# Tiles of the first pair beside the last batch: nine gathered instead of five, W_in earlier, W_out between the first units

## The chip, the core and the metric

The kernel runs on one core of a Trainium2 chip. The core has TensorE (PE, matrix products into PSUM), VectorE (DVE), ScalarE (ACT), GpSimd (POOL, which works on SBUF only) and SyncE (SP, which here issues every transfer). Each engine takes its instructions strictly in the order of its own queue and waits on semaphores for the others. The metric is the device time of one execution in microseconds (us), lower is better.

## What is computed

Three stages over 8 batches of 576 rows: an attention over 32 memory slots with 8 heads of 64, whose heads together are 512 columns; a first MLP of 512 to 2048 to 512 with a layer norm ahead and a residual; and a gated MLP. The change concerns the gated MLP and its loads:

```python
def _moe2_ref(x, w_in, g_ln, w_sg, b_sg, w_out):
    h = x @ w_in                                   # 512 -> 1024
    h = 0.5 * h * (1.0 + np.tanh(c * (h + 0.044715 * h ** 3)))
    u, v = (h[..., :d_ff // 2], h[..., d_ff // 2:])
    v_n = (v - mu) / np.sqrt(var + 1e-06) * g_ln   # over the 512 columns of v
    v_s = np.einsum('ts,bsd->btd', w_sg, v_n) + b_sg[None, :, None]
    gated = u * v_s
    return (x + gated @ w_out).astype(np.float32)
```

All weights and inputs arrive as 64-bit or 32-bit floats in DRAM. Products are made from pairs of a high and a low part (three matmuls for one), so every operand is converted and split into two tiles first.

## The kernel before

Phase 1 (`phase1`) is the attention and the first MLP. It goes through the batches one after the other. For each block of rows and each chunk c of the 2048 hidden columns `m1` makes a first-layer product into PSUM (ph, L550), `relu` splits it on ACT (hh, or cr for the 64 rows that belong to a tile shared with the next block, L536) and DVE (hl, L537), and three steps later `m2` adds the second-layer product into the PSUM tile of each row tile (py, L580 to L582). A finished row tile is scaled and added on DVE (L585) and stored to DRAM as y_d. The 36 row tiles have 128 rows; nine of them are a pair of batches, and the fifth of the nine (tile 4) holds 64 rows of each batch.

Phase 2 (`phase2`) is the gated MLP, pair by pair. For each row tile, y is loaded (`y_load`), transposed in blocks of 32 on DVE (`y_turn`, L824) and split (`y_split`: ACT L833, POOL L834). `s2` makes the v half of the first product (pv, 12 matmuls of 512 columns, L857), its gelu (ACT L843 square, DVE L844, ACT L845 tanh, DVE L846), the statistics over columns (DVE L867 to L869, reciprocal root on POOL L86 to L96), the scaling (DVE L871) and the split into vhl (ACT L874, POOL L875; for tile 4 in two parts L882, L883). Then there are 16 units of a pair: `s3` makes the u half (pu, 12 matmuls of 288 columns, L940) and its gelu; `s4` multiplies W_sg with all vhl of a batch (pvs, 14 matmuls of 288, L965), gates it (DVE L967, POOL L968) and splits it (ACT L970, POOL L971). In the loop the `s3` of a unit is written two units ahead of its `s4`. PSUM has two tiles for pu and two for pvs. `s5` makes the last product (po, L988), adds y (DVE L990) and stores.

W_in and W_out arrive as 64-bit floats. `load_piece` fetches a piece of 128 rows in two halves of 256 KB into tiles raw, of which there are three; `convert_piece` calls `split`: for each half ACT L108, DVE L109 and L110 make 32-bit floats of the words; for W_in ACT L122 and POOL L123 then make the two parts, for W_out, which is also scaled by 0.5, ACT L125 and DVE L126. Pieces 0 to 7 are W_in (its v half first), 8 to 11 W_out.

To keep PE busy at the change of phases, the table `ahead` hangs work of phase 2 on the steps of the last batch (`begin_phase2`): the chunks of W_sg, the pieces, and for the first five tiles of the first pair load, turn, split and `s2`. A list scheduler then orders each engine's instructions by its own estimate of when they are ready, so the order of instructions is not quite that of the code; the conversions, turns and splits carry an order edge (`issue_after`) behind the relu of the step.

## Time and profile before

| | us |
|---|---|
| median of 3 runs | 1232.28 |
| lowest and highest run | 1230.69, 1232.63 |
| the profiled execution | 1230.81 |
| its span, first to last instruction | 1229.0 |
| PE, DVE, ACT, POOL busy | 1182.6, 694.7, 467.4, 399.3 |
| mean granted clock of TensorE, share of full | 0.986 |

The last batch runs to about 805 us of the span, the gated MLP from there. PE matmuls overlap, so a busy time adds up ends that are modelled; how fast PE goes is read from the starts of its matmuls, one after the other. In a timeline row, what stands in brackets is the idle time ahead of the instruction and the instruction that ended it. An instruction's duration can hold a wait that no semaphore shows.

### The profile page before, as it was taken

The numbers are of one execution on the slowest core, as the hardware profiler recorded it, in microseconds if no ns is written. First come the engines' busy times: TensorE is split into PE (matmuls) and PEld (weight loads), VectorE is DVE, ScalarE is ACT, GpSimd is POOL, SyncE is SP. The second block draws the span as 40 slices with busy tenths as digits, with TensorE's granted clock in tenths as the row PEclk, the third lists the DMA queues.
The fourth block names the chain that finished last, engine by engine and source line by source line (L and its number), as shares of the span: only waits on it lengthen the run. The fifth ranks groups of instructions, "written<-read, shape, count | busy, mean of one in ns | idle before, by whom it ended". The sixth has DMA issues, their size and how long they took to land.

```text
span 1229.0 us, 20976 instructions
## 1 busy us (share of the span) xinstructions
PE 1182.6 (96%) x7711; PEld 988.0 (80%) x7711; DVE 694.7 (57%) x1669; ACT 467.4 (38%) x1064; POOL 399.3 (32%) x621
## 2 busy tenths in 40 slices
PE   4699899999999999999999999999999999999998
PEld 2376678878888778878878788788989988998997
DVE  2887565654744536645545545774576467447632
ACT  2565333223332323323223435543354354444430
POOL 2123212211211211201111103346586475657641
PEclk9699999999999999999999999999999999999999
DMA  9998764464534374343432233340141043023202
GB/s 207 270 247 244 196 177 111 102 167 124 138 94 120 89 217 87 97 141 82 125 119 70 71 98 104 94 132 1 52 140 42 10 127 97 1 70 95 78 18 69
DMA packets 204518, 138.85 MB, mean 113 GB/s; under 512 B 95104, under 2 KB 176128, under 8 KB 204416
## 3 DMA queue, kind: packets, MB, share of 16 engines
q1 hardware_dynamic: 204416, 137.51, 40.5%
q8 instruction: 61, 1.00, 0.3%
q14 instruction: 41, 0.34, 0.1%
HBM read 114.40 MB, written 31.33 MB: 119 GB/s over the span
## 4 chain that ended last, share of the span: by engine, by line
PE 82%; DVE 5%; DMA 5%; issue 3%; SPq 3%; ACT 1%; POOL 1%; DVEq 0%; POOLq 0%; ACTq 0%
PE ph L550 14%; PE pvs L965 10%; PE py L580 9%; PE py L582 9%; PE py L581 9%; PE po L988 8%; PE pu L940 8%; PE pv L857 7%; DMA raw<-in_moe_w_ch_dram 3%; SPq L81 3%; PE pvw L496 3%; PE kvp L294 2%; DMA q<-q_d 1%; PE sc L374 1%; PE px L430 1%
## 5 line engine op out<-in xcount | busy, mean ns | idle before, releaser
L550 PE MATMUL ph<-aTh,vw 128*128 128x320 f32 (+1 forms) x1024 | 246.4, 301 | 3.4 <-ACT vw L507 1.4
L580 PE MATMUL py<-whl,hh 128*128 128x512 f32 x512 | 205.9, 404 | 5.2 <-ACT hh L536 5.0
L581 PE MATMUL py<-whl,hh 128*128 128x512 f32 x512 | 203.3, 397 | 0.0
L550 PEld LDWEIGHTS ph<-aTh,vw 128*128 128x128 f32 x1024 | 177.9, 190 | 29.4 <-issue 8.3
L582 PE MATMUL py<-whl,hl 128*128 128x512 f32 x512 | 187.1, 397 | 0.0
L536 ACT ACTIVATE hh<-ph 128x256 fp32r<-128x256 f32 x256 | 97.5, 384 | 163.6 <-PE ph L550 95.5
L537 DVE SCALAR_TENSOR_TENSOR hl<-ph,hh 128x256 fp32r<-128x256 f32 x256 | 106.9, 422 | 91.4 <-ACT hh L536 89.5
L550 PE MATMUL ph<-aTl,vw 128*128 128x256 f32 (+1 forms) x512 | 152.8, 299 | 0.0
L965 PE MATMUL pvs<-wsh,vhl 128*128 128x288 f32 x576 | 123.5, 298 | 3.8 <-POOL vhl L883 2.7
L580 PEld LDWEIGHTS py<-whl,hh 128*128 128x128 f32 x512 | 97.0, 190 | 33.5 <-ACT hh L536 8.1
L581 PEld LDWEIGHTS py<-whl,hh 128*128 128x128 f32 x512 | 97.5, 190 | 19.8 <-issue 2.3
L940 PE MATMUL pu<-yTh,whl 128*128 128x288 f32 x512 | 111.3, 295 | 0.6 <-DVE ug L846 0.6
L550 PEld LDWEIGHTS ph<-aTl,vw 128*128 128x128 f32 x512 | 97.3, 190 | 10.3 <-issue 2.1
L582 PEld LDWEIGHTS py<-whl,hl 128*128 128x128 f32 x512 | 91.6, 189 | 15.8 <-issue 5.7
L965 PEld LDWEIGHTS pvs<-wsh,vhl 128*128 128x128 f32 x576 | 95.7, 190 | 5.6 <-POOL vhl L883 3.1
L857 PE MATMUL pv<-whl,yTh 128*128 128x512 f32 x288 | 90.9, 396 | 0.9 <-DVE vg L846 0.9
L988 PE MATMUL po<-whl,gh 128*128 128x512 f32 x288 | 90.0, 391 | 0.0
L940 PEld LDWEIGHTS pu<-yTh,whl 128*128 128x128 f32 x512 | 85.3, 188 | 2.0 <-DVE ug L846 1.0
L965 PE MATMUL pvs<-wsl,vhl 128*128 128x288 f32 x256 | 75.9, 297 | 0.0
L940 PE MATMUL pu<-yTl,whl 128*128 128x288 f32 x256 | 75.4, 294 | 0.0
L536 ACT ACTIVATE cr<-ph 128x64 fp32r<-128x64 f32 x128 | 28.4, 223 | 123.3 <-PE ph L550 122.8
L968 POOL TENSOR_TENSOR gt<-gt,ug 128x288 f32<-128x288 f32 x64 | 51.7, 809 | 65.1 <-DVE gt L967 64.9
(153 smaller groups left out, 2162.6 us busy)
## 6 DMA issues: line engine op xcount, KB each, us to landing
wc<-w_d SPq DMA_DIRECT2D x56, 512.0 KB, 4.9
y_d<-x SPq DMA_DIRECT2D x36, 256.0 KB, 2.7
yt<-y_d SPq DMA_DIRECT2D x36, 256.0 KB, 2.7
yr<-y_d SPq DMA_DIRECT2D x36, 256.0 KB, 3.0
kv<-in_k_dram SPq DMA_DIRECT2D x32, 256.0 KB, 4.0
kv<-in_v_dram SPq DMA_DIRECT2D x32, 256.0 KB, 4.2
raw<-in_moe_w_ch_dram SPq DMA_DIRECT2D x32, 256.0 KB, 8.3
raw<-in_moe_w_ch_dram SPq DMA_DIRECT2D x16, 512.0 KB, 7.4
```

Source lines behind the costliest of these rows:

```text
L81: return nc.sync.dma_start(out=out_ap, in_=in_ap)
L536: high = A.activation(out_h, src, AF.Relu)
L537: return high, V.scalar_tensor_tensor(out=out_l, in0=src, scalar=0.0, in1=out_h.bitcast(F32), op0=ALU.max, op1=ALU.subtract)
L550: PE.matmul(ph, w_[:, ks], x[:, g, 0:w], start=(n == 0), stop=(n == 3 * HK - 1))
L580: PE.matmul(py, hh, wh, start=start, stop=False)
L581: PE.matmul(py, hh, wl, start=False, stop=False)
L582: PE.matmul(py, hl, wh, start=False, stop=stop)
L857: PE.matmul(pv, y[:, kc, cs], w, start=(n == 0), stop=(n == 3 * KC - 1))
L940: PE.matmul(pu, w[:, ds_], y[:, kc, cs], start=(n == 0), stop=(n == 3 * KC - 1))
L965: PE.matmul(pvs, v_, w_, start=(n == 0), stop=(n == len(ops) - 1))
L968: G.tensor_tensor(out=gt, in0=gt, in1=ug, op=ALU.mult)
L988: PE.matmul(po, gg[:, dc, cs], w, start=(n == 0), stop=(n == 3 * KC - 1))
```

## The change

A constant `BESIDE = 7` is new. The table hangs only the eight pieces of W_in on the steps, each four steps sooner, and all nine tiles' load, turn and split, with `s2` for the first seven. The split pair of y tiles is allocated at the first `y_split` instead of the first `y_load`. W_out is loaded and converted in the loop of the first eight units, without the order edge; the two `s2` that are left stand behind the first and the third unit there.

```diff
     def convert_piece(p):
-        w = split(R.pop(("piece", p)), wpool, 0.5 if kind == 2 else None, R["relu"])
+        w = split(R.pop(("piece", p)), wpool, 0.5 if kind == 2 else None, None if kind == 2 else R["relu"])
...
-        if X["p"] == 0:
+        if X["p"] == 0 and t < BESIDE:
             z, vg = two(wpool, F32, "vg")
...
-            vh, vl = two(wpool if t < TPP - 2 else R["w3"], F32R, "vhl")
+            vh, vl = two(wpool if t < BESIDE else R["w3"], F32R, "vhl")
...
-    for n in range(len(PIECES)):
-        at_step(5 + 2 * n, load_piece, n)
-        at_step(7 + 2 * n, convert_piece, n)
-    for n in range(5):
-        at_step(18 + 2 * n, y_load, pairs[0], n)
-        at_step(20 + 2 * n, y_turn, pairs[0], n)
-        at_step(21 + 2 * n, y_split, pairs[0], n)
-        at_step(25 + 2 * n, s2, pairs[0], n)
+    for n in range(2 * KC):
+        at_step(1 + 2 * n, load_piece, n)
+        at_step(3 + 2 * n, convert_piece, n)
+    for n in range(TPP):
+        at_step(14 + 2 * n, y_load, pairs[0], n)
+        at_step(16 + 2 * n, y_turn, pairs[0], n)
+        at_step(18 + 2 * n, y_split, pairs[0], n)
+        if n < BESIDE:
+            at_step(20 + 2 * n, s2, pairs[0], n)
...
             if n == 0:
-                y_in(X, 5)
+                load_piece(2 * KC)
...
-                for t in range(5, TPP):
-                    if n == 0 and m == t - 5:
-                        s2(X, t)
-                        if t < TPP - 1:
-                            y_in(X, t + 1)
+                if n == 0 and m < 8:
+                    p, odd = divmod(m, 2)
+                    if odd:
+                        convert_piece(2 * KC + p)
+                        if p < KC - 1:
+                            load_piece(2 * KC + p + 1)
+                    elif p + BESIDE < TPP:
+                        s2(X, p + BESIDE)
```

The line numbers of the changed kernel are one or two higher (L874 is L875, L940 is L942, L967 is L969, L126 is L127). How the orders differ is shown at three places; up to the first conversion of W_in in the last batch, and again from the middle of the second pair on, they are the same.

ACT, near the end of the last batch, before: vhl is the cast of a gated tile, vg from pv its square, vg from vg its tanh, cr and hh are relu pieces, yTh the split of a y tile, raw and whl conversions of W_out.

```order
L874 CAST vhl_8871<-vg_8855 128x512
L125 ACTIVATE whl_8919<-raw_8838 128x256
L125 ACTIVATE whl_8919<-raw_8840 128x256
L843 ACTIVATE vg_8947<-pv_8934 128x512
L536 ACTIVATE cr_7926<-ph_8968 128x64
L845 ACTIVATE vg_8947<-vg_8947 128x512
L536 ACTIVATE hh_8975<-ph_8968 128x256
L536 ACTIVATE hh_8996<-ph_8989 128x256
L108 ACTIVATE raw_8930<-raw_8930 128x256
```

ACT, at the same first-layer products of the last batch, now.

```order
L875 CAST vhl_8887<-vg_8871 128x512
L844 ACTIVATE vg_8948<-pv_8935 128x512
L537 ACTIVATE cr_7926<-ph_8993 128x64
L846 ACTIVATE vg_8948<-vg_8948 128x512
L537 ACTIVATE hh_9000<-ph_8993 128x256
L834 CAST yTh_8657<-yb_8969 128x4x4x32
L537 ACTIVATE hh_9059<-ph_9052 128x256
L875 CAST vhl_8964<-vg_8948 128x512
L844 ACTIVATE vg_9025<-pv_9012 128x512
```

The conversions are gone from between, each tile has one split of a y tile beside it, and the cast of one gated tile stands directly ahead of the square of the next.

PE, at the entry of the gated MLP, before, from the end of the second u product on: pvs is the first gating product, which gets six of its 14 matmuls, and then comes pv of a further tile.

```order
L940 MATMUL pu_9235<-yTh_8625,whl_8707 128x288
L965 MATMUL pvs_9275<-wsh_8100,vhl_8871 128x288
L965 MATMUL pvs_9275<-wsl_8101,vhl_8871 128x288
L965 MATMUL pvs_9275<-wsh_8100,vhl_8871 128x288
L965 MATMUL pvs_9275<-wsh_8100,vhl_8963 128x288
L965 MATMUL pvs_9275<-wsl_8101,vhl_8963 128x288
L965 MATMUL pvs_9275<-wsh_8100,vhl_8963 128x288
L857 MATMUL pv_9295<-whl_8269,yTh_8625 128x512 x2
```

PE, at the same place, now: vhl_8887 and vhl_8964 are tiles 2 and 3, vhl_9041 is tile 4, pv_9321 tile 7.

```order
L967 MATMUL pvs_9301<-wsh_8100,vhl_8887 128x288
L967 MATMUL pvs_9301<-wsh_8100,vhl_8964 128x288
L967 MATMUL pvs_9301<-wsl_8101,vhl_8964 128x288
L967 MATMUL pvs_9301<-wsh_8100,vhl_8964 128x288
L858 MATMUL pv_9321<-whl_8157,yTh_8657 128x512 x2
L858 MATMUL pv_9321<-whl_8157,yTl_8658 128x512
L858 MATMUL pv_9321<-whl_8229,yTh_8657 128x512 x2
L858 MATMUL pv_9321<-whl_8229,yTl_8658 128x512
L858 MATMUL pv_9321<-whl_8299,yTh_8657 128x512
L967 MATMUL pvs_9301<-wsh_8100,vhl_9041 128x288
L967 MATMUL pvs_9301<-wz_8102,vhl_9041 128x288
```

The first gating product now runs through tiles 0 to 3 at once and takes tile 4 after seven matmuls of pv; before, the products of four more tiles (3 to 6) stood between its first six matmuls and the two that take tile 4.

DVE, from the fifth to the sixth gating (gt) of the first pair, before: z and ug are gelu pieces of u, vg and st belong to a gated tile.

```order
L967 SCALAR_TENSOR_TENSOR gt_9592<-pvs_9577,g2c_113,bb_9207 128x288
L846 SCALAR_TENSOR_TENSOR ug_9571<-z_9572,pu_9558 128x288
L868 BN_AGGR st_9390<-st_9390 128x2
L869 TENSOR_SCALAR st_9390<-st_9390 128x1
L87 TENSOR_SCALAR st_9390<-st_9390 128x1
L844 SCALAR_TENSOR_TENSOR z_9611<-z_9611,pu_9597 128x288
L846 SCALAR_TENSOR_TENSOR ug_9610<-z_9611,pu_9597 128x288
L871 TENSOR_SCALAR vg_9385<-vg_9385,st_9390 128x512
L967 SCALAR_TENSOR_TENSOR gt_9631<-pvs_9616,g2c_113,bb_9207 128x288
```

DVE, from the fifth gating of the first pair on, now.

```order
L969 SCALAR_TENSOR_TENSOR gt_9568<-pvs_9553,g2c_113,bb_9235 128x288
L110 TENSOR_SCALAR raw_9406<-raw_9406 128x256
L847 SCALAR_TENSOR_TENSOR ug_9547<-z_9548,pu_9534 128x288
L111 SCALAR_TENSOR_TENSOR raw_9406<-raw_9406 128x256
L110 TENSOR_SCALAR raw_9530<-raw_9530 128x256
L110 TENSOR_SCALAR raw_9532<-raw_9532 128x256
L111 SCALAR_TENSOR_TENSOR raw_9530<-raw_9530 128x256
L127 SCALAR_TENSOR_TENSOR whl_9519<-raw_9406,whl_9519 128x256
L111 SCALAR_TENSOR_TENSOR raw_9532<-raw_9532 128x256
L127 SCALAR_TENSOR_TENSOR whl_9612<-raw_9530,whl_9612 128x256
L127 SCALAR_TENSOR_TENSOR whl_9612<-raw_9532,whl_9612 128x256
L872 TENSOR_SCALAR vg_9461<-vg_9461,st_9466 128x512
```

The conversions of W_out stand between the gatings, in front of the next units' gelu pieces.

## Rows read from the trace of the kernel before

**Rows 1.** The page's part 1, busy us, share and instructions of PE.

```profile
PE 1182.6 (96%) x7711; PEld 988.0 (80%) x7711; DVE 694.7 (57%) x1669; ACT 467.4 (38%) x1064; POOL 399.3 (32%) x621
```

**Rows 2.** PE's timeline, end of the last batch: start us, us, operation, [idle before].

```profile
785.28 0.31 PE L550 MATMUL ph<-aTh,vw 128*128 128x320 f32 x1
...
786.88 0.40 PE L581 MATMUL py<-whl,hh 128*128 128x512 f32 x1
...
789.17 0.39 PE L582 MATMUL py<-whl,hl 128*128 128x512 f32 x1
790.46 0.50 PE L580 MATMUL py<-whl,cr 128*128 128x512 f32 x1 [0.90 <-ACT cr L536]
...
796.15 0.62 PE L857 MATMUL pv<-whl,yTh 128*128 128x512 f32 x2
```

**Rows 3.** ACT's timeline, last batch and start of the gated MLP.

```profile
788.54 0.62 ACT L874 CAST vhl<-vg 128x512 fp32r<-128x512 f32 x1 [4.02 <-DVE vg L871]
...
790.21 0.20 ACT L536 ACTIVATE cr<-ph 128x64 fp32r<-128x64 f32 x1
...
819.61 0.59 ACT L843 ACTIVATE vg<-pv 128x512 f32<-128x512 f32 x1
...
826.31 0.62 ACT L874 CAST vhl<-vg 128x512 fp32r<-128x512 f32 x1 [2.20 <-DVE vg L871]
```

**Rows 4.** PE's timeline, start of the gated MLP.

```profile
815.11 0.39 PE L857 MATMUL pv<-whl,yTl 128*128 128x512 f32 x1
...
835.31 0.40 PE L965 MATMUL pvs<-wsh,vhl 128*128 128x288 f32 x1 [2.66 <-POOL vhl L883]
...
841.15 0.62 PE L857 MATMUL pv<-whl,yTh 128*128 128x512 f32 x2
```

**Rows 5.** Stretches: PE, PEld, DVE, ACT, POOL busy; granted clock; DMA share; GB/s.

```profile
760.00:808.00 48.00, 46.06 (x232) 38.95 (x231) 34.57 (x73) 24.97 (x55) 20.22 (x24) 0.96 0.34 102
835.00:840.00 5.00, 4.34 (x20) 4.11 (x21) 4.06 (x11) 1.69 (x4) 4.85 (x7) 0.69 0.00 0
950.00:975.00 25.00, 25.00 (x190) 25.00 (x190) 10.24 (x22) 9.29 (x22) 13.98 (x20) 1.00 0.00 1
```

**Rows 6.** DVE's groups from 745 to 860 us: count, busy us, mean ns, idle before.

```profile
L824 DVE STREAM_TRANSPOSE yb<-yt 128x512 f32<-128x512 f32 x11 | 12.1, 1096 | 1.1 <-DMA yt<-y_d 1.1
...
L110 DVE SCALAR_TENSOR_TENSOR raw<-raw 128x256 uint32<-128x256 uint32 x16 | 6.6, 446 | 0.0
L126 DVE SCALAR_TENSOR_TENSOR whl<-raw,whl 128x256 fp32r<-128x256 f32 x8 | 6.2, 800 | 1.9 <-ACT whl L125 1.9
L109 DVE TENSOR_SCALAR raw<-raw 128x256 uint32<-128x256 uint32 x16 | 5.2, 366 | 0.9 <-DMA raw<-in_moe_w_out_dram 0.9
L867 DVE BATCH_NORM_STATS2 st<-vg 128x6 f32<-128x512 f32 x7 | 4.8, 686 | 0.0
L846 DVE SCALAR_TENSOR_TENSOR vg<-vg,pv 128x512 f32<-128x512 f32 x7 | 4.8, 686 | 3.3 <-ACT vg L845 3.3
...
L846 DVE SCALAR_TENSOR_TENSOR ug<-z,pu 128x288 f32<-128x288 f32 x9 | 3.9, 442 | 0.7 <-ACT z L845 0.6
...
L871 DVE TENSOR_SCALAR vg<-vg,st 128x512 f32<-128x512 f32 x7 | 3.8, 541 | 9.6 <-POOL st L96 9.6
L967 DVE SCALAR_TENSOR_TENSOR gt<-pvs,g2c,bb 128x288 f32<-128x288 f32 x7 | 3.5, 514 | 5.2 <-PE pvs L965 5.2
L585 DVE SCALAR_TENSOR_TENSOR x<-py,rs_t,x 128x512 f32<-128x512 f32 x5 | 3.5, 746 | 0.0
```

**Rows 7.** POOL's group of the split of tile 4, 745 to 860 us.

```profile
L883 POOL TENSOR_TENSOR vhl<-vg,vhl 64x512 fp32r<-64x512 f32 x2 | 2.5, 1264 | 1.4 <-ACT vhl L882 1.3
```

**Rows 8.** Timelines of POOL and of DVE at 777 us.

```profile
777.47 1.55 POOL L834 TENSOR_TENSOR yTl<-yb,yTh 128x512 fp32r<-128x512 f32 x1 [5.69 <-ACT yTh L833]
...
777.63 1.67 DVE L126 SCALAR_TENSOR_TENSOR whl<-raw,whl 128x256 fp32r<-128x256 f32 x1 [0.70 <-ACT whl L125]
```

**Rows 9.** Transfers: engine, count, KB each, median us from issue to landing.

```profile
raw<-in_moe_w_out_dram SPq DMA_DIRECT2D x8, 256.0 KB, 2.7
```

More of the change, by code (lines that the diff above doesn't have):

```diff
@@ L51, in fused_kernel @@
     LAG = 3
+    BESIDE = 7
     SCALE = 1.0 / math.sqrt(D)
@@ L804, in y_load @@
     def y_load(X, t):
-        if t == 0:
-            X["yT"] = (
-                R["py"].tile([P, KC, TPP * P], F32R, tag="yTh", name="yTh"),
-                R["py"].tile([P, KC, TPP * P], F32R, tag="yTl", name="yTl"),
-            )
         if R.get("p2") is None:
@@ L826, in y_split @@
     def y_split(X, t):
+        if t == 0:
+            X["yT"] = (
+                R["py"].tile([P, KC, TPP * P], F32R, tag="yTh", name="yTh"),
+                R["py"].tile([P, KC, TPP * P], F32R, tag="yTl", name="yTl"),
+            )
         yh, yl = X["yT"]
```

## The prediction

> **What bounds the kernel now.** I read the page's busy shares first, then TensorE's own timeline for places where it waits, then the timeline of the engine that it waited for, then the groups of instructions for prices. TensorE (PE) is busy for 96% of the span [rows 1], so a gain can only come from time in which it stands still, or runs at the lower of its two clock levels, and all other work counts only where it makes PE do so. After the start of the kernel nearly all of that time lies in two places, and the change touches both.
>
> The first is in the last batch [rows 2]. From 789.17, the end of a run of second-layer products, to 796.15, the first pv, are 6.98 us, with 12 matmuls of 512 columns. The ten between 786.88 and 789.17 go at 0.23 us each, so 12 are 2.8 us of work, and **4.2 us are lost**: waits for relu pieces (the first 0.90) and slow matmuls after them. Who made PE wait is seen on ScalarE (ACT) [rows 3]: before 788.54 it stood 4.02 us at the cast of a gated tile (vhl, L874) for DVE's L871, and the relu piece cr, which PE wanted, came only behind it, at 790.21. ACT and DVE had the conversions of W_out in their queues there besides.
>
> The second is the start of the gated MLP [rows 4]. From 815.11 to 841.15 are 26.04 us, with 25 matmuls of 512 columns and 87 of 288. At 0.23 and at 0.132 (190 in 25 us in [rows 5]) that is 5.75 + 11.5 = 17.3 us of work: **8.8 us are lost**. The longest wait, 2.66, is for the split of tile 4 (vhl, L883), and from 835 to 840 the granted clock is 0.69 [rows 5], a part of the stretch at 1.2 GHz: 0.31 x 5 = 1.5 of the 8.8.
>
> So 4.2 + 8.8 = 13.0 us can be won here at most.
>
> **The change part by part.** The profiled execution took 1230.81 us (span 1229.0, 1.81 outside it). The median of the runs is 1232.28, 1.47 above it; I work on the first and add 1.47 at the end.
>
> *W_in four steps sooner.* The same 16 loads and 32 ACT, 32 DVE and 16 POOL instructions move from the crowded end of the last batch towards its beginning, under the first-layer and second-layer products of those steps. The first three halves are loaded long before in both kernels, since there are three buffers, so SP's order changes only behind them; SP waits there for freed buffers, with W_sg loads and y stores queued behind it, and none of these is wanted for many steps. I price it at 0; if the cover fails, one late relu piece costs what it did at the first stall, 0.9 [rows 2].
>
> *W_out out of the last batch, six products before the units instead of three.* Five of W_out's eight halves leave the last batch wholly, the other three with their second part (L125, L126). The order shows the products of tiles 0 to 5 ahead of the first unit, and tile 6 only behind the first gating product, so six and not seven. This takes away what made both old stalls: **-13.0**. What comes instead:
>
> (a) *The chain of one gated tile.* ACT takes square, tanh and cast of a tile in order, and the square of tile t+1 stands behind the cast of tile t (fence on ACT). In the trace that chain, from a square at 819.61 to the end of its cast at 826.93, is 7.3 us with little between [rows 3]; in the last batch DVE puts a transpose of 1.10 in it [rows 6], so 8.4. PE's work for one tile there is 27 matmuls of 512 columns (12 pv, 15 py) and 12 of the first layer in 1.60 us [rows 2]: 6.2 + 1.6 = 7.8. ACT then falls back by 0.6 a tile over the last three tiles, 1.8 in all (the order has more PE work between the first three). By the order PE reads a relu piece no less than 2.1 us of matmuls behind its first-layer product, so between 0 and the lag, 1.8, is lost; near the lower end, since the lag and the piece itself (0.20 [rows 3]) together fit 2.1: 0.5.
>
> (b) *Tile 4 at the entry.* On DVE its last scaling (L871) stands behind four L585: 4 x 0.75 + 0.54 [rows 6], then two casts of 0.62 (as L874 [rows 3]) and the first POOL piece, 1.26 [rows 7]: 6.0, and some 0.5 of hand-overs. PE has 36 matmuls of 288 columns and 7 of 512 before it wants the piece: 4.75 + 1.6 = 6.4. So 0.1 short; bounds 0 and the old 2.66 [rows 4]; I take 0.2.
>
> (c) *W_out between the first units.* This is the dear part (last pair of fences). From the fourth gating (L967) to the eighth DVE has 5 gatings of 0.51, 7 gelu pieces of 0.44, 8 of L126 and 5 of L110 at 0.45, 5 of L109 at 0.37, two transposes of 1.10, one L871 and 0.5 of small ones [rows 6]: 2.6 + 3.1 + 3.6 + 2.2 + 1.8 + 2.2 + 0.5 + 0.5 = 16.5 us. It starts late, since two L871, a gelu end (L846 vg), a gelu piece and statistics (L867) stand ahead: 1.1 + 0.7 + 0.4 + 0.7 = 2.9. PE's work from the end of the fourth unit's product to the end of the eighth's is 92 matmuls of 288 and 5 of 512, 13.3 us, and it needs the eighth gating only when it wants that PSUM buffer again, two units later: 5.5 more. So 19.4 against 18.8, nearly even *if* L126 costs no more than L110, which has its shape and its operation. It does: 0.80 in the mean [rows 6], and one took 1.67 beside a POOL instruction of 1.55 that had begun just before it [rows 8]. So 8 x 0.35 = 2.8 more; POOL was busy 0.42 of the stretch where these ran and is 0.56 in a stretch of units [rows 5], 2.8 x 0.56/0.42 = 3.7. DVE then is late by 19.4 + 3.7 - 18.8 = 4.3. Besides, the last five halves of W_out wait for one of three load buffers, freed by an L126, with a landing (2.7 us [rows 9]) between, and ACT and DVE wait for it in line, the next units' gelu behind it: 0 to 2.7, I take 1.0. **(c) 5.3**, bounds 0.6 (no meeting with POOL) and 8 (a meeting for twice the mean at L126, and a full landing).
>
> (d) *The clock.* The fall after the old waits cost 1.5 at one place. New waits are shorter and spread: 0 to 3.0, I take 0.8.
>
> On SP the W_out loads now stand between the residual loads and the next pair's y tiles, and wait for L126; those y tiles are wanted only after the sixteenth unit, so 0.
>
> Sum: 13.0 - (0.5 + 0.2 + 5.3 + 0.8) = 6.2 won; 1230.81 - 6.2 = 1224.6, and with 1.47 **1226.1 us**.
>
> The Trainium skill ("SBUF — State Buffer", "SBUF: two separate sides") says that DVE and GpSimd share a pair of ports under an exclusive lock, held for a whole instruction, and that a DVE instruction with two SBUF inputs takes part in it. The long L126 agrees with that, and the rule speaks against putting this work where POOL is busier; the third rival is the same mechanism at its full price.
>
> **The rivals.** *W_out hides* (more won): if (c) costs 1.0 or less, and (d) nothing, 13.0 - 1.7 = 11.3 are won: 1221.0. For it: DVE's plain work in (c) nearly fits (19.4 against 18.8). Against: the measured L126.
>
> *The chain sets the pace* (no change): PE waits for the chain in (a) at five tiles, about 1.0 each, and runs slowly for 1.5 in the sequel, 6.5 instead of 0.5; then 13.0 - 12.8 is nothing, 1232.1. For it: the order of ACT still holds relu pieces behind a cast, as in the first stall. Against: DVE has far less beside it now, and the lag of 1.8 is about what PE's lead takes up.
>
> *The port* (slower): each of the 18 DVE instructions of W_out in (c) meets a POOL instruction. At 1.0 each (the worst seen was 1.67 - 0.45 = 1.2) DVE has 19.4 + 18 against 18.8, 18.6 lost, with 1.0 for landings, 0.7 from (a) and (b) and 1.5 for the clock 21.8 against 13.0: 1241.1. It decides from new losses of 15.5, that is from 0.65 apiece; L126 had 0.35 in the mean, the other two less.
>
> **How the numbers follow.** About 0.2% (2.5 us) is what can be told from no change. Forecast 1226.1, with (c) from 2 to 8 1223 to 1229: chance 0.50. W_out hides, around 1221: 0.24. The chain, around 1232: 0.15. The port, 1235 and above: 0.11. So faster 0.74, same 0.15, slower 0.11. The range 1220 to 1233 takes in all but the port and the edges.
>
> **What would show it.** Right: no PE wait above 0.5 us in the 40 us ahead of the gated MLP, none above 1 for L883, the clock at 1.00 there; instead PE waits of 0.5 to 2 us for DVE's L846 or L967 some 30 to 50 us after the first unit starts, with L126 lengthened beside POOL. (a) is wrong if waits for cr or hh stay in the last batch. (c) is wrong if W_out's stretch shows no PE wait, or more than 8 us of them. The whole is wrong if PE's own work grows, of which the order gives no sign: its matmuls are the same, moved.

## The result and the profile after

The changed kernel takes **1218.82 us** in the median of 6 runs (1216.53 to 1222.72), the kernel before 1232.26 in the 6 runs beside it: a ratio of 0.9892, 95% interval 0.9875 to 0.9909. The forecast was 1226.1 with a range from 1220.0 to 1233.0: the sign was right, the gain was about twice the 6.2 us forecast, and the median lies 1.2 us below the range. The rival nearest to it is *W_out hides*, at 1221.0. One of the ten runs of e2 below took 1268.2 us at a granted clock of 0.89, where its others had 0.98 or more, and is left out of its median and its ratio.

The profiled execution took 1216.53 us (span 1214.7). PE's line of the page's part 1, to be held against [rows 1]:

```profile
PE 1176.8 (97%) x7711; PEld 985.0 (81%) x7711; DVE 692.4 (57%) x1669; ACT 467.0 (38%) x1064; POOL 400.3 (33%) x621
```

The counts of instructions are the same; work was only moved. Two of the stretches of [rows 5], in the trace of after (PE, PEld, DVE, ACT, POOL busy; granted clock; DMA share; GB/s):

```profile
760.00:808.00 48.00, 48.00 (x242) 40.88 (x241) 28.09 (x62) 20.73 (x38) 24.24 (x36) 1.00 0.12 35
835.00:840.00 5.00, 5.00 (x39) 4.91 (x38) 4.56 (x13) 3.11 (x9) 4.83 (x9) 1.00 0.45 154
```

PE fills the 48 us that hold the end of the last batch, where it had 46.06, and the clock, 0.96 there and 0.69 from 835 to 840 before, is 1.00 (the 2.4 GHz level) in both. From 740 to 900 us the view of waits names nothing for PE; before, the same stretch had nine lines there, the longest 2.66 for L883 [rows 4].

**How much of the gain is the change's.** The kernel up to the last batch, with a start where transfers are busy for over 0.9 of the first 120 us, is the same program before and after, yet PE comes to its first transpose of W_sg (ptw, the first work of phase 2 in the last batch) at a different time. PE's timelines, of before:

```profile
702.37 0.60 PE L783 MATMUL ptw<-ident,ws 128*128 128x128 f32 x4
```

of after:

```profile
699.92 0.60 PE L784 MATMUL ptw<-ident,ws 128*128 128x128 f32 x4
```

From there to the span's end are 1229.0 - 702.37 = 526.6 us before and 1214.7 - 699.92 = 514.8 after. So **11.8 us** are won by what was changed, and 2.45 of the 14.3 between the two profiled executions lie in the start. I use span less this transpose below; it has much less noise than the times.

Where the 11.8 lie is read from the starts of PE's matmuls: what each takes to the next, less what its kind takes when PE is full (0.23 us for 512 columns, 0.133 for 288). In this sum, from the first W_sg transposes to 900 us:

| lost by PE, us | before | after |
|---|---|---|
| last batch | 5.3 | 1.7 |
| first 25 us of the gated MLP | 3.2 | 0.0 |
| the units behind it | 4.9 | 0.7 |
| sum | 13.4 | 2.4 |

The difference is 11.0; 0.8 of the 11.8 is not located. In before's last batch 1.1 of the 5.3 lies outside the stall, in pieces below 0.25 us.

**The last batch, after.** ACT's timeline (the cast of gated tiles, L875, the relu pieces cr, L537), against [rows 3]:

```profile
773.41 0.22 ACT L537 ACTIVATE cr<-ph 128x64 fp32r<-128x64 f32 x1 [0.28 <-PE ph L551]
...
789.67 0.59 ACT L844 ACTIVATE vg<-pv 128x512 f32<-128x512 f32 x1
...
797.28 0.62 ACT L875 CAST vhl<-vg 128x512 fp32r<-128x512 f32 x1 [4.13 <-DVE vg L872]
797.80 0.59 ACT L844 ACTIVATE vg<-pv 128x512 f32<-128x512 f32 x1
798.53 0.22 ACT L537 ACTIVATE cr<-ph 128x64 fp32r<-128x64 f32 x1
```

and on PE, for the first and for the last of these four tiles, the last first-layer matmul (ph) ahead of the relu piece and the product that reads this cr, against [rows 2]:

```profile
773.07 0.31 PE L551 MATMUL ph<-aTh,vw 128*128 128x320 f32 x1
...
776.95 0.39 PE L581 MATMUL py<-whl,cr 128*128 128x512 f32 x1
...
798.19 0.31 PE L551 MATMUL ph<-aTh,vw 128*128 128x320 f32 x1
...
800.43 0.40 PE L581 MATMUL py<-whl,cr 128*128 128x512 f32 x1
```

ACT still stands 4 us at the cast, and the relu piece still comes behind it. But here it is not late: it starts 0.34 us behind the start of the last first-layer matmul ahead of it at both tiles (773.41 - 773.07, 798.53 - 798.19), and it is ready before PE wants it, 776.95 - 773.63 = 3.3 us ahead at the first tile and 800.43 - 798.75 = 1.7 ahead three tiles on. The idle time on ACT is the same as in the old stall; the lead is what differs.

**The entry.** Tile 4's split on POOL, against [rows 7], and PE's products of tile 4 (wz is read with tile 4 alone), against [rows 4]:

```profile
810.10 2.65 POOL L884 TENSOR_TENSOR vhl<-vg,vhl 64x512 fp32r<-64x512 f32 x2 [1.89 <-ACT vhl L883]
```

```profile
812.87 0.40 PE L858 MATMUL pv<-whl,yTh 128*128 128x512 f32 x1
813.11 0.29 PE L967 MATMUL pvs<-wsh,vhl 128*128 128x288 f32 x1
813.24 0.29 PE L967 MATMUL pvs<-wz,vhl 128*128 128x288 f32 x1
```

The first of the two pieces ends near 811.4, 1.7 us before PE asks for it; no idle time stands behind the row at 813.11, where before had 2.66.

**W_out between the first units.** DVE's timeline from the fourth gating of the first pair (832.85) to the eighth (L969), cut to the rows that the reading uses, and POOL's beside it; in DVE's rows L127 is L126 of before, L110 was L109:

```profile
832.85 0.50 DVE L969 SCALAR_TENSOR_TENSOR gt<-pvs,g2c,bb 128x288 f32<-128x288 f32 x1
833.27 1.09 DVE L127 SCALAR_TENSOR_TENSOR whl<-raw,whl 128x256 fp32r<-128x256 f32 x3
...
836.32 0.88 DVE L110 TENSOR_SCALAR raw<-raw 128x256 uint32<-128x256 uint32 x1
...
839.85 1.36 DVE L127 SCALAR_TENSOR_TENSOR whl<-raw,whl 128x256 fp32r<-128x256 f32 x2
...
850.18 0.47 DVE L969 SCALAR_TENSOR_TENSOR gt<-pvs,g2c,bb 128x288 f32<-128x288 f32 x1
```

```profile
833.43 1.59 POOL L970 TENSOR_TENSOR gt<-gt,ug 128x288 f32<-128x288 f32 x1 [0.45 <-DVE gt L969]
...
836.23 0.82 POOL L973 TENSOR_TENSOR gl<-gt,gh 128x288 fp32r<-128x288 f32 x1
...
839.64 0.96 POOL L973 TENSOR_TENSOR gl<-gt,gh 128x288 fp32r<-128x288 f32 x1
```

The same stretch in the view of busy times, and two of DVE's groups from 820 to 870 us (count, busy us, mean ns, idle before):

```profile
832.85:850.65 17.80, 17.66 (x129) 17.13 (x128) 15.82 (x38) 9.17 (x24) 12.12 (x16) 1.00 0.41 133
```

```profile
L127 DVE SCALAR_TENSOR_TENSOR whl<-raw,whl 128x256 fp32r<-128x256 f32 x8 | 3.9, 523 | 0.0
L110 DVE TENSOR_SCALAR raw<-raw 128x256 uint32<-128x256 uint32 x5 | 3.1, 642 | 1.0 <-DMA raw<-in_moe_w_out_dram 0.9
```

DVE needs 17.8 us from gating to gating, where the forecast had 21.2 and a late start of 2.9 besides. L127 has 0.52 in the mean, not the 0.80 of [rows 6]; L110 has 0.64 where that group (then L109) had 0.37.

### The profile page after: what moved, and what is told of

It is laid out like the page before. It is cut to its first block, busy times and chain, and to the rows that moved or that the text cites. A ratio compares the mean times of both kernels' runs of the same rounds, so it can differ in the third digit from the quotient of the medians.

```text
span 1214.7 us, 20985 instructions
## 1 busy us (share of the span) xinstructions
PE 1176.8 (97%) x7711; PEld 985.0 (81%) x7711; DVE 692.4 (57%) x1669; ACT 467.0 (38%) x1064; POOL 400.3 (33%) x621
## 4 chain that ended last, share of the span: by engine, by line
PE 86%; DVE 4%; DMA 4%; SPq 3%; issue 1%; ACT 1%; POOL 1%; DVEq 0%; POOLq 0%; ACTq 0%
PE ph L551 16%; PE py L583 10%; PE py L581 10%; PE py L582 10%; PE pvs L967 8%; PE po L990 8%; PE pv L858 8%; PE pu L942 7%; SPq L82 3%; PE pvw L497 3%; DMA raw<-in_moe_w_ch_dram 2%; PE kvp L295 2%; DMA q<-q_d 1%; PE sc L375 1%; PE px L431 1%
## 5 line engine op out<-in xcount | busy, mean ns | idle before, releaser
L537 ACT ACTIVATE hh<-ph 128x256 fp32r<-128x256 f32 x256 | 97.7, 384 | 164.5 <-PE ph L551 95.8
L967 PE MATMUL pvs<-wsh,vhl 128*128 128x288 f32 x576 | 120.8, 294 | 0.0
L942 PE MATMUL pu<-yTh,whl 128*128 128x288 f32 x512 | 111.0, 295 | 0.2
L583 PEld LDWEIGHTS py<-whl,hl 128*128 128x128 f32 x512 | 91.7, 189 | 15.9 <-issue 5.7
L967 PEld LDWEIGHTS pvs<-wsh,vhl 128*128 128x128 f32 x576 | 94.1, 188 | 0.6
L942 PEld LDWEIGHTS pu<-yTh,whl 128*128 128x128 f32 x512 | 85.1, 188 | 1.7 <-DVE ug L847 0.7
L942 PE MATMUL pu<-yTl,whl 128*128 128x288 f32 x256 | 75.4, 295 | 0.0
L967 PE MATMUL pvs<-wsl,vhl 128*128 128x288 f32 x256 | 75.4, 295 | 0.0
L970 POOL TENSOR_TENSOR gt<-gt,ug 128x288 f32<-128x288 f32 x64 | 52.8, 826 | 68.4 <-DVE gt L969 65.6
L537 ACT ACTIVATE cr<-ph 128x64 fp32r<-128x64 f32 x128 | 28.4, 223 | 116.8 <-PE ph L551 116.1
```

The source lines that it names most:

```text
L537: high = A.activation(out_h, src, AF.Relu)
L583: PE.matmul(py, hl, wh, start=False, stop=stop)
L942: PE.matmul(pu, w[:, ds_], y[:, kc, cs], start=(n == 0), stop=(n == 3 * KC - 1))
L967: PE.matmul(pvs, v_, w_, start=(n == 0), stop=(n == len(ops) - 1))
L970: G.tensor_tensor(out=gt, in0=gt, in1=ug, op=ALU.mult)
```

## Experiments

Each was run beside the kernel before. The numbers, with the lost time by starts as in the table above:

| kernel | median us | ratio to before, 95% interval | span less transpose | last batch | entry | units |
|---|---|---|---|---|---|---|
| before | 1232 | 1 | 526.6 | 5.3 | 3.2 | 4.9 |
| after | 1218.8 | 0.9892 [0.9875, 0.9909] | 514.8 | 1.7 | 0.0 | 0.7 |
| after_again | 1221.5 | 0.9907 [0.9883, 0.9931] | 514.8 | 1.4 | 0.0 | 0.4 |
| e1 W_out late, tiles as before | 1222.8 | 0.9922 [0.9892, 0.9951] | 518.2 | 3.4 | 0.0 | 1.8 |
| e2 W_out in the last batch | 1225.0 | 0.9940 [0.9923, 0.9957] | 518.5 | 6.0 | 0.0 | -0.2 |
| e3 L127 twice | 1224.9 | 0.9934 [0.9913, 0.9955] | 520.2 | 1.6 | 0.0 | 6.2 |
| e4 before, POOL in halves | 1229.9 | 0.9985 [0.9971, 1.0000] | 524.6 | 1.3 | 6.7 | 4.2 |
| e6 W_in as before | 1221.9 | 0.9906 [0.9881, 0.9932] | 516.0 | 2.0 | 0.0 | 1.6 |
| e7 two more tiles in the units | 1220.8 | 0.9912 [0.9891, 0.9933] | 514.6 | 1.5 | 0.1 | 0.3 |
| e8 L127 half twice | 1221.1 | 0.9914 [0.9897, 0.9931] | 515.1 | 1.3 | 0.1 | 0.9 |
| e9 low part on POOL | 1223.1 | 0.9929 [0.9912, 0.9946] | 514.9 | 1.4 | 0.0 | 0.2 |
| e9_again | 1219.4 | 0.9890 [0.9866, 0.9914] | 515.0 | 1.6 | 0.0 | 0.8 |
| e10 low part on POOL, in the last batch | 1221.6 | 0.9913 [0.9882, 0.9943] | 516.2 | 3.5 | 0.1 | -0.1 |

### Which part of the change made which gain

**e1: W_out between the units, but W_in and the tiles as before.** Edit against the changed kernel:

```diff
-        at_step(1 + 2 * n, load_piece, n)
-        at_step(3 + 2 * n, convert_piece, n)
-    for n in range(TPP):
-        ... (all nine tiles, seven s2)
+        at_step(5 + 2 * n, load_piece, n)
+        at_step(7 + 2 * n, convert_piece, n)
+    for n in range(5):
+        at_step(18 + 2 * n, y_load, pairs[0], n)
+        ... (as before; s2 of tiles 5 to 8 between the first units)
```

> Only the move of W_out between the first units is kept; W_in, and the five tiles beside the last batch, stand at the steps of the kernel before. Theory 1 (the first stall came from W_out's conversions in the queues of ACT and DVE; the second from tiles gathered too late): the loss in the last batch falls from 4.2 to 1 us or less, but the entry of the gated MLP still waits for tile 4 and now has W_out on DVE besides, so 8 to 11 us are lost there; 1228 to 1231 us. Rival (the first stall is the chain of square, tanh and cast of one tile, whoever else is in the queue): 3 to 4 us stay lost in the last batch, and the time is 1231 to 1235.

Measured: span less transpose 518.2, so 8.5 of the 11.8 us are won with W_out's move alone; 3.4 are lost in the last batch, nothing at the entry, 1.8 in the units. That the entry would keep its old loss was wrong: without W_out beside them the five tiles reach the first gating in time. The old stall of the last batch is gone as well; what is lost there now lies elsewhere, in two waits of 0.7 us behind 780.95. The first, in the view of waits (PE's product, what it waited for, us in all, times, longest), and DVE's timeline ahead of the instruction that it waited for:

```profile
PE py L583 <- DVE cr L538: 0.7, 1, 0.7
```

```profile
780.84 1.09 DVE L820 STREAM_TRANSPOSE yb<-yt 128x512 f32<-128x512 f32 x1 [2.61 <-DMA yt<-y_d]
```

DVE stood 2.6 us at the turn of a y tile, for its load, and the relu's low part stood behind it; the second wait is for a relu piece that stood on ACT behind the split of the same tile. Why this load came late was not followed up. The one long wait in the units is a last-layer product that comes before W_out is converted (the view of waits):

```profile
PE po L989 <- ACT whl L126: 1.5, 1, 1.5
```

**e2: the other half alone.** The tiles and W_in as in the changed kernel, W_out's pieces behind W_in's in the last batch, with their order edge:

```diff
-    for n in range(2 * KC):
+    for n in range(len(PIECES)):
         at_step(1 + 2 * n, load_piece, n)
         at_step(3 + 2 * n, convert_piece, n)
...
-                    if odd:
-                        convert_piece(2 * KC + p)
-                        ...
-                    elif p + BESIDE < TPP:
+                    if not odd and p + BESIDE < TPP:
                         s2(X, p + BESIDE)
```

> The changed kernel with W_out's four pieces put back into the last batch, directly behind W_in, with their order edge. Theory 1: DVE then has 2.2 us a piece more between the tiles there, L126 meets POOL's instructions of 1.3 to 1.6 us again (0.7 us or more in the mean), PE loses 2 to 5 us in the last batch, and the entry and the units stay clean: 1221 to 1224. Rival (nine tiles earlier is all that counts, W_out's place nothing): below 1 us lost, 1218 to 1220.

Measured: 518.5, 8.2 us won; the entry and the units lose nothing, the last batch loses 6.0, 4.3 more than after and more than the 2 to 5 expected. So **W_out's conversions beside the gated tiles cost the last batch 4.3 us**, and they made the old stall, which went with them in e1; the loss at the entry goes with either half. The two largest of PE's waits, 740 to 900 us:

```profile
PE py L581 <- ACT hh L537: 1.2, 2, 0.9
PE py L583 <- DVE cr L538: 1.2, 2, 0.7
```

Each half alone wins 8.2 to 8.5; together 11.8, not 16.7, since both take away the loss at the entry and much of that behind it.

**e6: W_in four steps later again, the rest as in the changed kernel.**

```diff
-        at_step(1 + 2 * n, load_piece, n)
-        at_step(3 + 2 * n, convert_piece, n)
+        at_step(5 + 2 * n, load_piece, n)
+        at_step(7 + 2 * n, convert_piece, n)
```

> The changed kernel with W_in's eight pieces at the steps of the kernel before, four steps later, so that the last four pieces stand beside the first tiles' turns and products. Theory: each piece is 1.3 us of DVE and 1.5 of POOL in two steps of 5 to 8 us, beside 5.2 us of DVE for a tile; 0 to 1.5 us are lost in the last batch, 1219 to 1220.5. Rival (the four steps are what frees the last batch): 3 to 4 us lost there, 1222 to 1223.

Measured: 516.0, so W_in's earlier place is worth 1.2 us, 0.9 of it seen in the units. The forecast priced it at 0, as something that costs nothing; it brings a little.

### How near the edge W_out stands between the units

**e3: L127 computed twice for every half.**

```diff
+                V.scalar_tensor_tensor(out=l, in0=w, scalar=scale, in1=h.bitcast(F32), op0=ALU.mult, op1=ALU.subtract)
                 V.scalar_tensor_tensor(out=l, in0=w, scalar=scale, in1=h.bitcast(F32), op0=ALU.mult, op1=ALU.subtract)
```

> The changed kernel with each of the eight low parts of W_out (DVE L127) computed twice, 8 x 0.5 = 4 us more on DVE between the first units, none elsewhere. If DVE's work there (17.8 us from the fourth gating to the eighth, 1.1 us ahead of the moment when PE wants the buffer) has no room left, as the predicted sum had it, 2.5 to 4 us more are lost by PE: 1221.5 to 1223. Rival (the stretch has more room, since DVE's idle 2.0 us and the planner's order give way): under 0.8 us, 1219 to 1219.8.

Measured: 520.2, 5.4 us more than after (2.5 to 4 were expected), all of it in the units. The 16 instructions took 9.97 us by their means (0.80 and 0.45) where the eight took 4.18. PE's waits from 800 to 900 us, and the stretch behind them:

```profile
PE pu L943 <- DVE ug L848: 2.1, 1, 2.1
PE po L991 <- DVE whl L128: 1.7, 1, 1.7
```

```profile
850.00:870.00 20.00, 16.37 (x104) 15.79 (x105) 14.82 (x29) 6.58 (x17) 7.90 (x10) 0.91 0.30 92
```

The two waits are 3.8 us, and a clock of 0.91 over 20 us (0.18 of it at 1.2 GHz) is another 1.8: 5.6, against 5.4 measured. So with 5.8 us more of this work DVE sets the pace of the stretch: term (c) had the right engine, and this much on top costs what the prediction thought the change itself would cost.

**e8: L127 twice for the second half of each piece alone.**

```diff
+                if i == 1:
+                    V.scalar_tensor_tensor(out=l, in0=w, scalar=scale, in1=h.bitcast(F32), op0=ALU.mult, op1=ALU.subtract)
                 V.scalar_tensor_tensor(out=l, in0=w, scalar=scale, in1=h.bitcast(F32), op0=ALU.mult, op1=ALU.subtract)
```

> The changed kernel, with L127 computed twice for the second half of each piece of W_out only: four more instructions of about 0.5 us, 2 us more DVE work between the first units. Theory, DVE had 0.4 us of room there (0.6 late and 17.8 us against 18.8): 1.5 to 2.5 us more lost in the units, 1220.5 to 1221.5, in line with the 5.4 for twice as many. Rival, PE's waits have a threshold of their own further off (a wait brings the clock down only when it is long): 0 to 0.7 us, 1219 to 1219.5.

Measured: 515.1, 0.2 more than after: not the 1.5 to 2.5 expected, and no proof of room either, since one wait of 0.7 us for DVE's ug came back. The four instructions were added, but DVE's groups show that others became shorter:

```profile
L127 DVE SCALAR_TENSOR_TENSOR whl<-raw,whl 128x256 fp32r<-128x256 f32 x8 | 3.1, 413 | 0.0
L129 DVE SCALAR_TENSOR_TENSOR whl<-raw,whl 128x256 fp32r<-128x256 f32 x4 | 2.6, 662 | 0.0
...
L110 DVE TENSOR_SCALAR raw<-raw 128x256 uint32<-128x256 uint32 x5 | 1.8, 362 | 0.7 <-DMA raw<-in_moe_w_out_dram 0.7
```

L127 with L129 takes 5.95 by the means, 1.8 more than in after, and L110 1.4 less. The meetings with POOL had moved (see e11), so the run says less on the room than it was meant to.

**e7: two more gated tiles between the units instead of beside the last batch.**

```diff
-        if n < BESIDE:
+        if n < 5:
             at_step(20 + 2 * n, s2, pairs[0], n)
...
-                    elif p + BESIDE < TPP:
-                        s2(X, p + BESIDE)
+                    else:
+                        s2(X, p + 5)
```

> The changed kernel, but only five of the nine gathered tiles are made beside the last batch and four (not two) between the first units. Theory, DVE is full there with W_out: two more tiles bring it 2 x (0.69 + 0.69 + 0.69 + 0.54) = 5.2 us more of work, and PE 2 x 12 products of 512 columns, 5.6 us of cover, of which the last batch no longer has; the gelu chain of a tile in line with the units' gelus costs 3 to 5 us of new waits: 1222 to 1224. Rival, the tiles' own work carries their cover with it: no more than 1 us lost, 1219 to 1220.

Measured: 514.6, no loss, though L127 took 0.87 us in the mean:

```profile
L127 DVE SCALAR_TENSOR_TENSOR whl<-raw,whl 128x256 fp32r<-128x256 f32 x8 | 6.8, 866 | 1.2 <-ACT whl L126 1.2
```

My expectation was wrong, and the rival right: with the tiles, 24 matmuls of 512 columns (24 x 0.23 = 5.5 us) moved to the same place, and that cover holds DVE's work. From the fourth gating to the eighth are 23.1 us there, instead of 17.8. How many tiles go ahead, five or seven, is of no weight once W_out is out of the last batch.

**e9, e9_again: the low part of W_out on POOL.** ACT scales by 0.5 and POOL subtracts, so DVE loses L127.

```diff
-                A.activation(h, w, AF.Copy, scale=scale)
-                V.scalar_tensor_tensor(out=l, in0=w, scalar=scale, in1=h.bitcast(F32), op0=ALU.mult, op1=ALU.subtract)
+                A.activation(w, w, AF.Copy, scale=scale)
+                A.copy(h, w)
+                G.tensor_tensor(out=l, in0=w, in1=h.bitcast(F32), op=ALU.subtract)
```

> The changed kernel with the low part of W_out made by POOL: ACT scales the 32-bit floats by 0.5 in place, casts the high part, and POOL subtracts, so DVE loses eight L127 (4.2 us) between the first units, ACT gets 8 x 0.3 us more and POOL 8 x 0.8 us. Theory, DVE alone sets what is lost in the units: the 0.7 us lost there go, 1218. Rival, POOL at 0.68 busy becomes the late one (its pieces of the gated halves are what the last products wait for) or its instructions lengthen DVE's: 1 us or more lost in the units, 1219 to 1222.

> The kernel with W_out's low part on POOL between the first units, again, on the same chip as the changed kernel. Its trace lost 0.5 us less than the changed kernel behind the first transpose, yet its median was 4.2 us higher, in another job. Theory, the 4.2 lie in the start and vary: the two kernels' medians come within 2 us of each other. Rival, it is slower somewhere that the starts of matmuls do not show: 3 to 5 us above the changed kernel again.

Measured: 514.9 and 515.0 less the transpose, the same as after; 0.2 and 0.8 us lost in the units. Nothing more was to be had there, since only 0.4 to 0.7 was left; and DVE lost the eight L127, but its L111 took 0.69 in the mean where after has 0.41, with POOL busier beside it. The first median lies above both expectations. The medians, 1223.1 and then 1219.4 for the same kernel, lie on both sides of after's.

**after_again: the changed kernel a second time.**

> The changed kernel, unchanged, beside the kernel before and the next one, to see whether its median holds. Theory, the start of the kernel (the first 120 us, where transfers set the pace) differs from run to run by some us whatever the kernel: the median comes to 1218 to 1222 and the first W_sg transpose anywhere between 699 and 705 us; span less that start again 514.3 to 515.5. Rival, the start belongs to the kernel: 1217.5 to 1219.5, transpose at 699.5 to 700.5.

Measured: 1221.49 (1220.51 to 1223.06) beside 1231.79 for before. The first transpose of its profiled execution:

```profile
706.54 0.60 PE L784 MATMUL ptw<-ident,ws 128*128 128x128 f32 x4
```

That is 6.6 us later than in the first profile of the same program, and 1221.3 - 706.54 = 514.8 behind it is the same to 0.1. The start varies by more than half of what the change brings. The ten runs of after have a median of 1220.7, 11.6 below the 1232.3 of before, and that agrees with the 11.8 read behind the transpose; the 13.4 of the first comparison holds some 2 us of the start.

### What lengthens L126

**e4: the kernel before, POOL's instructions beside W_out in halves.**

```diff
-        G.tensor_tensor(out=lv, in0=yb, in1=hv.bitcast(F32), op=ALU.subtract)
+        for n in range(1 if R.get("p2") else 2):
+            bs = slice(0, 4) if R.get("p2") else slice(2 * n, 2 * n + 2)
+            G.tensor_tensor(out=lv[:, bs], in0=yb[:, bs], in1=hv[:, bs].bitcast(F32), op=ALU.subtract)
...
-            G.tensor_tensor(out=vl, in0=vg, in1=vh.bitcast(F32), op=ALU.subtract)
+            ... (the same for vl, in halves of 256 columns)
```

> The kernel before, with two POOL instructions of the last batch each cut into two halves (the low part of a y tile, L834, and of a gated tile, L875), so that POOL has the same elements to do in pieces of about 0.8 us instead of 1.3 to 1.6. Question: by what does the wait of L126 beside POOL go? Theory, by the length of the POOL instruction that it meets: L126's mean falls from 0.80 us to 0.6 or less, the loss of PE in the last batch falls from about 5.3 to 2.5 to 4.5, the median is 1230 to 1232. Rival, by POOL's busy share, as the prediction scaled it: POOL is as busy as before or more, so L126 stays at 0.75 to 0.85, and the time at 1232 to 1234.

Measured: L126 fell from 0.80 to 0.71 only, between the two expectations, and the time by 0.15%, which is at the edge of the noise. As a test it failed, for two reasons. The planner ordered the rest of the stretch anew (the first u product came at 799.86 us instead of 804.86), so that the loss went from the last batch (5.3 to 1.3) to the entry (3.2 to 6.7). And two L126 in a row met two POOL halves in a row, DVE's timeline and POOL's:

```profile
788.03 1.61 DVE L126 SCALAR_TENSOR_TENSOR whl<-raw,whl 128x256 fp32r<-128x256 f32 x2 [0.88 <-ACT whl L125]
```

```profile
787.74 1.62 POOL L879 TENSOR_TENSOR vhl<-vg,vhl 128x256 fp32r<-128x256 f32 x2 [1.31 <-ACT vhl L876]
```

The pair takes 1.6 as it does behind one whole POOL piece, and ends 789.64 - 789.36 = 0.28 behind the second half. That number led on. In the traces of before, after, e2, e3 and e7, wherever an L126 or L127 begins while a longer POOL instruction (0.8 us and up) that began ahead of DVE's row of them is under way, it ends 0.27 to 0.29 behind POOL's end, and one queued behind it 0.33 to 0.34 later; where it begins first it takes 0.41. In after: 839.64 + 0.96 = 840.60 is the end of POOL's piece, and the L127 that had begun at 839.85 ended at 840.88, a single one of 1.03. It goes the other way round too: the three L127 from 833.27 began ahead of POOL's L970 at 833.43, took 0.42 each, and L970 took 1.59 where its median is 0.81, ending 0.66 behind the last of them (835.02, 834.36). L970 at 847.33, begun 0.16 behind an L127, took 0.91 and ended 0.66 behind it as well.

**e11: the meeting by itself.** Behind the end of the changed kernel, trials one after the other: ACT releases a POOL instruction and then, by a copy of chosen length, a DVE instruction.

```diff
+    A.copy(ua, sa)
+    G.tensor_tensor(out=sa[:, 0:512], in0=sa[:, 0:512], in1=ua[:, 0:512], op=ALU.subtract)
+    A.copy(va[:, 0:64], ua[:, 0:64])        # 64, 256, 512 or 2 x 512 columns: the delay
+    V.scalar_tensor_tensor(out=da[:, 0:256], in0=da[:, 0:256], scalar=0.5, in1=va[:, 0:256], op0=ALU.mult, op1=ALU.subtract)
```

> The changed kernel with a trial of the port behind its end, one case after the other (the time of the whole grows by some 40 us and says nothing): ACT releases a POOL subtraction of 512 columns (1.3 us; one case 256, 0.8), then copies 64, 256, 512 or twice 512 columns and so releases a DVE instruction of 256 columns 0.25 to 1.5 us later; the same without POOL's. Theory, from the starts and ends of L126 and L127 in the traces: a DVE instruction with two SBUF inputs that begins while a POOL instruction is under way ends 0.28 us behind that one's end, and takes its own 0.41 when it begins behind it. So about 0.41 without POOL, 1.3 at a delay of 0.25, 1.2 at 0.35, 0.9 at 0.65, 0.41 at 1.5, and 0.8 beside 256 columns. For a tensor_scalar with one SBUF input: ends 0.16 behind POOL's. With the other input in PSUM, and for a copy: unknown for the copy, no wait for PSUM (L846, L847 showed none). Rival, a share of the bandwidth: each takes longer by the same 0.3 to 0.5 us wherever in POOL's instruction it begins, and is not tied to POOL's end.

POOL's timeline, five of the trials:

```profile
1221.30 1.26 POOL L1054 TENSOR_TENSOR sa<-sa,ua 128x512 f32<-128x512 f32 x1 [1.34 <-ACT ua L1053]
1223.91 1.26 POOL L1059 TENSOR_TENSOR sa<-sa,ua 128x512 f32<-128x512 f32 x1 [1.34 <-ACT ua L1058]
1226.52 1.27 POOL L1064 TENSOR_TENSOR sa<-sa,ua 128x512 f32<-128x512 f32 x1 [1.34 <-ACT ua L1063]
...
1236.06 1.26 POOL L1084 TENSOR_TENSOR sa<-sa,ua 128x512 f32<-128x512 f32 x1 [2.92 <-ACT ua L1083]
1240.24 1.26 POOL L1093 TENSOR_TENSOR sa<-sa,ua 128x512 f32<-128x512 f32 x1 [2.92 <-ACT ua L1092]
```

DVE's, the instruction of each of these trials, ahead of them one without POOL (1217.81):

```profile
1217.81 0.36 DVE L1046 SCALAR_TENSOR_TENSOR da<-da,va 128x256 f32<-128x256 f32 x1
...
1221.53 1.31 DVE L1056 SCALAR_TENSOR_TENSOR da<-da,va 128x256 f32<-128x256 f32 x1 [1.01 <-ACT va L1055]
...
1224.30 1.15 DVE L1061 SCALAR_TENSOR_TENSOR da<-da,va 128x256 f32<-128x256 f32 x1 [1.18 <-ACT va L1060]
...
1227.12 0.94 DVE L1066 SCALAR_TENSOR_TENSOR da<-da,va 128x256 f32<-128x256 f32 x1 [1.39 <-ACT va L1065]
...
1236.22 1.24 DVE L1086 TENSOR_SCALAR va<-va 128x256 f32<-128x256 f32 x1 [1.01 <-ACT va L1085]
...
1240.41 0.42 DVE L1095 SCALAR_TENSOR_TENSOR da<-va,pa 128x256 f32<-128x256 f32 x1 [1.01 <-ACT va L1094]
```

The first three end at 1222.84, 1225.45 and 1228.06, each 0.27 to 0.28 behind POOL's end (1222.56, 1225.17, 1227.79), though they began 0.23, 0.39 and 0.60 into it. With a delay past POOL's end it took 0.43. A tensor_scalar with one SBUF input ended 0.14 behind POOL's end (alone it took 0.29), a copy 0.15; with one input in PSUM there was no wait, 0.42 with POOL and 0.42 without. So **the instruction waits out what is left of POOL's instruction, whole**; it is no share of anything, and the rival falls.

That also bears on why before had its meetings, three in eight L126. ACT's timeline of before, the row behind the cast of [rows 3] at 788.54:

```profile
789.07 0.75 ACT L125 ACTIVATE whl<-raw 128x256 fp32r<-128x256 f32 x2
```

with POOL's and DVE's rows:

```profile
789.25 1.27 POOL L875 TENSOR_TENSOR vhl<-vg,vhl 128x512 fp32r<-128x512 f32 x1 [1.31 <-ACT vhl L874]
```

```profile
789.53 1.60 DVE L126 SCALAR_TENSOR_TENSOR whl<-raw,whl 128x256 fp32r<-128x256 f32 x2 [1.02 <-ACT whl L125]
```

ACT's cast releases POOL, and ACT's next instruction releases DVE 0.28 later: with one ACT queue ahead of both, this meeting is made by the order, not by chance. The one of [rows 8] came about in the same way, 0.16 behind POOL's start, and in e2 all three later pairs, at 0.29. The third in before (807.35 on DVE, 807.15 on POOL) did not: there both engines came late, from other work.

**e10: e2, with the low part on POOL as in e9.** The edits are those of e2 and e9 together.

> W_out back in the last batch (as in the run that had its conversions there), but its low part made by POOL and not by DVE, ACT getting a scaling of 0.3 us more for each half. In the trace of that run three pairs of L127 began 0.29 us behind the start of a POOL piece of a gated tile, and each pair took 1.6 us instead of 0.8. Theory, these meetings on DVE (2.5 us) with L127's own 3.3 us made the last batch's loss of 6.0: it falls to 2 to 3.5, and span less start is 515.5 to 517. Rival, the queue of ACT made it (conversions between the gelu pieces and the relu pieces): with 2.4 us more on ACT the loss is 5.5 to 7.5, and span less start 518.5 to 520.5.

Measured: the last batch loses 3.5 instead of 6.0, span less transpose is 516.2. The waits of PE that are left, 740 to 900 us:

```profile
PE py L582 <- ACT hh L538: 0.9, 1, 0.9
PE py L584 <- DVE cr L539: 0.3, 1, 0.3
```

So L127 and its meetings on DVE made 2.5 of the 4.3 us that W_out costs in the last batch; most of the waiting that is left (0.9 of 1.2) is for ACT, which has more work in this run. That ACT's queue makes the whole of the rest is not shown.

## Why the prediction fell short

- **What could be won, 13.0:** near. The losses by starts are 13.4 before, and 1.1 of them were not in the two stalls. Both stalls are gone, for the reasons given: e1 and e2 take the halves apart.
- **(a), 0.5 for the chain on ACT:** the size is near, but PE did not wait for the chain. From the square at 789.67 to the end of the next cast, 797.90, are 8.2 us, where 8.4 was worked out, and PE's tiles follow at 7.83 (776.95 to 800.43 are three), where 7.8 was forecast. But at the first two of the four squares ACT still waited for PE's pv (0.68 and 0.74 us), so it had that much in hand, and the relu piece cr never fell back: 0.34 behind its matmul at the first tile and at the fourth. That the lead falls from 3.3 to 1.7, by 1.6, where a lag of 1.8 was worked out, is chance: it is PE's own order, which has 3.9 us between the first-layer matmul and the product at the first tile and 2.2 at the fourth. By starts the last batch lost 0.3 to 0.6 beyond the 1.1 (1.7 and 1.4 in two traces), with no wait of 0.25 us or more: near the 0.5, but not by a wait for the chain.
- **(b), 0.2 for tile 4:** 0; it was ready 1.7 us early.
- **(c), 5.3 for W_out between the units:** this is the step that failed. What was lost there is 0.7 and 0.4 in two traces, with (d). The forecast set 2.9 + 16.5 + 3.7 + 1.0 = 24.1 us against 18.8 of room; in the trace it is 0.6 + 17.8 = 18.4, which just fits: the eighth gating ended at 850.65, and PE came back to its PSUM buffer at 851.30. Term by term:
  - The late start, from the end of the fourth gating product (832.23) to the gating at 832.85, was 0.6 instead of 2.9. The two L871, the gelu end and the statistics do stand ahead of the fourth gating, but DVE did them from 830.37 on, beside PE's product, 13 of whose 14 matmuls ran from 830.34 to 832.2.
  - The plain work was counted well but added up wrongly. The 36 instructions from the fourth gating to the eighth take 18.2 us by their durations, 15.9 without the lengthening priced below (16.5 was forecast), yet DVE was busy for 15.8 in all: 30 of them start some 0.08 us before the end of the one ahead. Three L127 of 0.42 take 1.09, not 1.26. In all that is 2.4 us.
  - The meetings at L126 were priced at 3.7 by POOL's busy share. They were 0.9: two of eight met. POOL's share did rise, to 12.12 of 17.80, 0.68, and L127 still got shorter: the scaling by share was the wrong law. A meeting costs what is left of POOL's instruction, and whether there is one goes largely by what releases both. In the units L127 stands behind other DVE work and no longer right behind the cast that releases POOL.
  - In return L110 met POOL three times in five: 0.64 each, 1.4 us over the 0.37 that was priced. And DVE stood idle for 2.0, where the landings had 1.0. Together, 24.1 - 2.3 - 0.6 - 2.4 - 2.8 + 1.4 + 1.0 = 18.4.
- **(d), 0.8 for the clock:** 0; with no long wait it stayed at 1.00. In e3, where waits of 2.1 and 1.7 came back, it fell to 0.91.
- **The bound of 8 for (c)** is not what its terms come to: 0.6, twice 2.8 for the meetings and a full landing of 2.7 are 8.9. Nothing hangs on it here.
- **The offset of 1.47** from the profiled execution to the median was right in kind and small beside the start's variation.

With 0.7 for (c) and (d), 0.6 for (a) and 0 for (b), 13.0 - 1.3 = 11.7 is the sum, and 11.8 was measured behind the transpose; that it comes so close is in part luck, since 0.8 of the 11.8 is not located. The low end of the range, 1220.0, was *W_out hides* with little spare: it left out the start, which in the first comparison gave some 2 us, and the median of the ten runs, 1220.7, lies just inside it. That does not save the forecast: the 11.6 won there are still near twice 6.2, and (c) is why. *W_out hides* was the rival that came true, with (c) at 1.0 or less and (d) at nothing. The *port* rival had the right mechanism and the wrong premise, that each instruction meets one. As for the *chain*, PE waited for no relu piece.

By the prediction's own list: no PE wait above 0.5 ahead of the gated MLP, none for L883 and a clock of 1.00 came as said; the waits of 0.5 to 2 us for L846 or L967 did not come, which it had named as the sign that (c) is wrong. In e3 one comes, of 2.1, for the instruction that is L846 here (ug, L848 there).

## What to carry to other kernels

When an engine's work is weighed against another's, take its busy time over a stretch or the distance from start to start, not a sum of mean durations, and count the work that stands ahead from when its inputs are there. A lengthened DVE instruction is to be laid beside POOL's timeline: if it ends a fixed step behind POOL's end, it is a meeting, worth what is left of POOL's instruction. What to look at then is what releases the two; cutting POOL's pieces in halves did not take the meetings away (e4). And where a kernel's start depends on transfers, compare two profiles from the first work behind it, before a microsecond is explained.

## What the runs showed of the hardware

A DVE instruction of 256 columns that reads SBUF alone stood still until POOL's instruction under way had ended, and ended 0.27 to 0.28 us behind it with two inputs, 0.14 to 0.15 for a tensor_scalar or a copy with one; with one input in PSUM it took 0.42 with and without POOL (e11). The Trainium skill ("SBUF — State Buffer", "SBUF: two separate sides") calls this an exclusive lock held for the whole instruction, which DVE takes with two SBUF inputs (against a GpSimd instruction that reads SBUF) or in a two-port mode; these rows agree, though no run here shows in which mode the tensor_scalar and the copy ran. The other direction stands in the trace of after: POOL's L970, which takes 0.81 in the median, ended 0.66 us behind the last L127 that had come before it, once for three of them in a row (1.59 in all) and once for one (0.91).

The same program reached its first W_sg transpose at 699.92 us in one execution and at 706.54 in another. It is not the change: three kernels with that same start, run beside each other, came there at 701.93 (e9_again), 702.85 (e10) and 706.54 (after_again). Why the start varies by so much was not settled; transfers were busy for 0.91 of the first 120 us in both.
